# Attention with memory and a two-layer block on one core: more load buffers, and another split of the first queries' preparation over the engines

## The chip, the core and the metric

The kernel runs on one core of a Trainium2 chip. The core has TensorE (PE in the profile) for matrix products, VectorE (DVE), ScalarE (ACT) and GpSimd (POOL) for work on elements, and SyncE (SP), whose queue issues most of the transfers. The metric is the device time of one execution in microseconds, as the median of several runs.

## What is computed

Four batches, eight heads, 576 tokens, head width 64. The output of attention, 2304 tokens of 512 values, passes through a two-layer block with 2048 hidden values.

```python
scores = where(causal, -1e9, q @ k.T / 8);  a = softmax(scores);  local = a @ v
q_p = where(q > 0, q, exp(q) - 1) + 1
mem_out = (q_p @ M_prev) / (q_p @ z_prev + 1e-6)
g = 1 / (1 + exp(-beta))
x = g * mem_out + (1 - g) * local          # (4, 576, 8*64) in all
h = x @ w_in
out = (h * sigmoid(1.702 * h)) @ w_out
```

## The kernel before

Heads are handled in pairs: two heads of 64 channels fill 128 partitions, and a batch has four pairs, 16 pairs in all. Attention of the 16 pairs, the first product of the block (x by `w_in`, 16 blocks of 128 columns, 8 chunks of tokens) and the second product (with `w_out`) follow each other on TensorE, with the first product's matmuls filling in between those of attention.

*The first queries.* `first_queries` (L286) handles the first 256 queries of batch 0 for all four pairs at once, so that the block has a first chunk x to work on early. It loads keys and queries (`fk`, `fq`, `fv`, `fm`, `fz`: keys and queries transposed, queries, values, memory, normaliser). `score` computes scores, their row maximum (VectorE, L541) and exp (ScalarE, L547). `norm` (L339) scales the exp by the reciprocal of their sum, one head on GpSimd and one on VectorE (L550), transposes them on TensorE (L351 to L353) and copies them out on ScalarE into `ft`. `phi` (L361) computes q_p: ScalarE makes exp(-relu(-q)) into `fqm`, and max(q, 0) is added to it, for two pairs on VectorE in one operation (L369), for the other two on GpSimd in two (L368, L370); then q_p is multiplied by z, for two pairs on VectorE, for two on GpSimd. `phin` (L380) sums that over the channels, takes the reciprocal and divides q_p by it, again two pairs on each engine. `mscale` (L375) multiplies the memory by the gate g, one operation a pair on GpSimd. `qtr` transposes the divided queries and copies them to `fqt`; `values` (L400) multiplies everything with memory and values, and `split_sum` turns the result into the two parts `xh` and `xl` of x. The order of calls is norm(0), phi, norm(1), phin, norm(2), norm(3), mscale, qtr, values.

*The weights.* A block of `w_in` comes as pairs of 32-bit words of a 64-bit number (`wraw`, 512 KB). `conv_unit` (L200) loads it, scales it on ScalarE (L213), puts the bits together in three VectorE operations (L224, L229, L231) and splits the result into `wi` (ScalarE, L236, and GpSimd, L241). The raw words of the 16 blocks use the buffers named by the letters in `conv_in` (L268): `c` has two of its own, `e` two of a pool used later for `w_out`, `h` and `l` those of x of later batches. Blocks 0 to 3 are loaded at the start, the others at slots before their place in `CONV`. The decoding of block 0 is told to stay behind the division of pair 1 and the last VectorE scaling (`state["bits"]`).

*The rest of the pairs.* Work is put into slots by `at(slot, priority, fn)`; pair p begins at slot `K0[p]` (7 or 8 slots apart). `load_kq` and `load_vq` issue the transfers of a pair on SyncE's queue: keys and queries transposed (`kqf`, two buffers), values (`vr`, two buffers), memory, queries and normaliser (`mr`, `qr`, `zb`, pool `ldp`, one buffer each). `plan_prep` computes q_p from `qr` in `qmin` and `qexp` (ScalarE, L489, L492), `qphi` (VectorE, L496), `zmul` (GpSimd), `norm` and `smul`, and scales the memory in `mplain`. Within a queue or engine instructions run in the order in which a planner puts them when the program is built; it weighs readiness by a model of time and the priorities, and `add_manual_dep` with `NOSYNC` fixes the order of two instructions on one engine. The planner orders the whole program at once.

Of the kernel before, what the change touches and what calls it, by code (L numbers as in the profile page):

```python
# [34 lines left out]
def tile_attention_memory_moe(ctx, tc, kq, vq, mem, zz, beta, w_in, w_out, out):  # L35
# [29 lines left out]
    mox = pool(attn, "mox", 2, side="right")  # L65
    ldp = pool(attn, "ldp", side="right")
    att = pool(attn, "att", side="right")
    wkp = pool(attn, "wkp", side="right")
    sml = pool(attn, "sml", 6, side="right")
    ps_s = pool(attn, "ps_s", 4, space=PSUM, side="right")  # L70
    ps_x = pool(attn, "ps_x", 1, space=PSUM, side="right")
# [196 lines left out]
    def conv_in(blk):  # L268
        w = w1[blk].tile([128, 2, DM], F32R, name=f"wi{blk}")
        if blk < AHEAD:  # L270
            wb[blk] = w
        raw = {
            "c": (cnv, {"bufs": 2}), "e": (ear[0], {"tag": "r"}),
            "h": (mop, {"tag": "xh"}), "l": (mop, {"tag": "xl"})}["cceehlcchleeccee"[blk]]
        ws = (lambda: ps_o, {"tag": "po"}) if blk == 3 else (lambda: ps_x, {"tag": "ps"})
        parts = conv_unit(None, w, w_in[blk], *raw, *ws, att, {"tag": f"qpt{blk % 2}", "bufs": 2})
        if blk < AHEAD:
            return parts

        c = CONV[blk - AHEAD]  # L280
        at(max(c - 6, -7), 58, parts[0])
        for fn in parts[1:]:
            at(c, 58, fn)
        at(c + 3, 1, lambda: wb.update({blk: w}))

    def first_queries(b):  # L286
# [74 lines left out]
        def phi(behind):  # L361
# [4 lines left out]
            nc.scalar.activation(out=w, in_=w, func=AF.Exp, scale=-1.0)  # L366
            v, p = slice(0, NP), slice(NP, 2 * NP)
            nc.gpsimd.tensor_scalar(out=qv[:, p], in0=qv[:, p], scalar1=0.0, scalar2=None, op0=ALU.max)  # L368
            nc.vector.scalar_tensor_tensor(out=qv[:, v], in0=qv[:, v], scalar=0.0, in1=w[:, v], op0=ALU.max, op1=ALU.add)  # L369
            tt("P", qv[:, p], qv[:, p], w[:, p], ALU.add)  # L370
            for c in range(NP):
# [3 lines left out]
        def mscale(c):  # L375
            x = nc.gpsimd.tensor_scalar(
                out=m[:, c], in0=m[:, c], scalar1=gt[:, c:c + 1], scalar2=None, op0=ALU.mult)
            tc.add_manual_dep(x.ins, box["n", min(c + 1, 3)], NOSYNC, reason="fm")

        def phin():  # L380
            n = fst.tile([128, NP, 2, 2, 1], F32, name="fn")
            nv = n.rearrange("p c t h o -> p (c t) h o")
            nc.vector.tensor_reduce(out=nv[:, :, :, 0], in_=qm, op=ALU.add, axis=AX.X)
            nc.vector.reciprocal(out=n, in_=n)
            for c in range(NP):
                w = q[:, c].rearrange("p t (h d) -> p t h d", h=2)
                box["q", c] = tt("VP"[c // 2], w, w, n[:, c].to_broadcast([128, 2, 2, D]), ALU.mult).ins.name

# [31 lines left out]
        norm(1)  # L420
        phin()
        norm(2)
        norm(3)
        state["bits"] = (box["q", 1], box["v", 3])
        for c in range(NP):
# [25 lines left out]

    def load_vq(p):
        b, c = pairs[p]

        vr = att.tile([128, 5, 128], F32, name="vr", bufs=2)
        nc.sync.dma_start(vr, vq[b, c, :, 0])
        mr = ldp.tile([128, 2, D], F32, name="mr")
# [5 lines left out]
        nc.sync.dma_start(zb, zz[b, c:c + 1, :].to_broadcast([128, 128]))  # L463
        raws[p].update(v=vr, m=mr, q=qr, z=zb)

# [5 lines left out]
    def plan_prep(p):  # L471
# [62 lines left out]
        if p + 1 < len(pairs):  # L534
            at(K0[p + 1] - 11, 60, lambda: load_kq(p + 1))
            at(max(K0[p + 1] - 8, s0 + 8), 60, lambda: load_vq(p + 1))

# [275 lines left out]
    load_kq(0)  # L813
    load_vq(0)
    for p in range(NPAIRS):
# [326 lines left out]
```

## Time and profile before

| what | us |
|---|---|
| median of 3 runs (615.55 to 618.78) | 615.9 |
| the profiled execution, its own time | 616.93 |
| its span from first to last instruction | 615.2 |
| TensorE busy | 593.0 (96%) |
| VectorE busy | 421.7 (69%) |
| ScalarE busy | 347.9 (57%) |
| GpSimd busy | 214.9 (35%) |

All times in the rows below are counted from the start of the profiled span. An engine that is busy all the time sets the pace of its stretch; where it stands, the view of waits tells what it stood for. The granted clock is TensorE's, as a share of 2.4 GHz. A wait that several things end is put down to the one that came last.

### The profile page before, as it was taken

The numbers are of one execution on the slowest core, as the hardware profiler recorded it, in microseconds if no ns is written. First come the engines' busy times: TensorE is split into PE (matmuls) and PEld (weight loads), VectorE is DVE, ScalarE is ACT, GpSimd is POOL, SyncE is SP. The second block draws the span as 40 slices with busy tenths as digits, with TensorE's granted clock in tenths as the row PEclk, the third lists the DMA queues.
The fourth block names the chain that finished last, engine by engine and source line by source line (L and its number), as shares of the span: only waits on it lengthen the run. The fifth ranks groups of instructions, "written<-read, shape, count | busy, mean of one in ns | idle before, by whom it ended". The sixth has DMA issues, their size and how long they took to land.

```text
span 615.2 us, 11404 instructions
## 1 busy us (share of the span) xinstructions
PE 593.0 (96%) x4000; PEld 518.4 (84%) x4000; DVE 421.7 (69%) x1022; ACT 347.9 (57%) x811; POOL 214.9 (35%) x279
## 2 busy tenths in 40 slices
PE   5789999999999999999999999999999999999997
PEld 3467767777787888787788889999999999999997
DVE  5877986666667576676565434679688679766964
ACT  6776766555557355365454343465686865576441
POOL 4765665543536235344334231213412401220000
PEclk9598999999999999999999999999999999999999
DMA  8784442433255355365342126522544733471002
GB/s 261 266 282 119 164 140 92 133 125 104 71 178 189 91 173 173 85 198 151 108 135 66 54 74 221 194 92 75 182 149 138 250 118 75 144 245 52 26 1 77
DMA packets 46985, 84.11 MB, mean 137 GB/s; under 512 B 5328, under 2 KB 33232, under 8 KB 46928
## 3 DMA queue, kind: packets, MB, share of 16 engines
q1 hardware_dynamic: 40688, 61.36, 30.5%
q0 software_dynamic: 6240, 22.02, 11.5%
q8 instruction: 31, 0.51, 0.4%
q14 instruction: 26, 0.21, 0.1%
HBM read 59.77 MB, written 23.59 MB: 136 GB/s over the span
## 4 chain that ended last, share of the span: by engine, by line
PE 68%; DVE 10%; issue 6%; DMA 6%; ACT 5%; POOL 3%; SPq 0%; DVEq 0%; POOLq 0%; ACTq 0%
PE pm L129 22%; PE acc L994 20%; PE ps L129 9%; PE pt L138 8%; PE po L129 8%; DVE wo L151 2%; DMA g<-gd 2%; DMA qr<-in_vq_dram 2%; POOL g L937 2%; ACT a L547 2%; DVE ps L541 1%; DVE st L151 1%; DMA wraw<-in_w_out_dram 1%; DMA wraw<-in_w_in_dram 1%; DVE ol L151 1%
## 5 line engine op out<-in xcount | busy, mean ns | idle before, releaser
L129 PE MATMUL pm<-xh,wi 128*128 128x320 f32 (+1 forms) x1024 | 219.7, 305 | 1.5 <-POOL wi L151 1.4
L129 PEld LDWEIGHTS pm<-xh,wi 128*128 128x128 f32 x1024 | 165.5, 190 | 7.5 <-POOL wi L151 2.7
L994 PE MATMUL acc<-oh,wo 128*128 128x384 f32 x672 | 169.6, 336 | 0.7 <-ACT hk L143 0.7
L129 PE MATMUL pm<-xl,wi 128*128 128x256 f32 (+1 forms) x512 | 152.1, 298 | 0.1
L994 PEld LDWEIGHTS acc<-oh,wo 128*128 128x128 f32 x672 | 121.4, 188 | 1.3 <-ACT hk L143 1.0
L550 POOL TENSOR_SCALAR a<-a,sm,g 128x512 f32<-128x512 f32 (+3 forms) x112 | 76.3, 693 | 129.4 <-DVE sm L601 97.6
L994 PE MATMUL acc<-ol,wo 128*128 128x384 f32 x336 | 111.0, 337 | 0.4 <-DVE ol L151 0.4
L151 DVE TENSOR_TENSOR ol<-g,oh 128x768 fp32r<-128x768 f32 x84 | 79.6, 954 | 40.1 <-ACT oh L143 39.8
L129 PEld LDWEIGHTS pm<-xl,wi 128*128 128x128 f32 x512 | 96.9, 190 | 0.5 <-DVE xl L151 0.3
L547 ACT ACTIVATE a<-ps,nm 128x256 f32<-128x256 f32 (+2 forms) x112 | 59.7, 539 | 64.2 <-DVE nm L541 64.1
L143 ACT ACTIVATE oh<-g 128x768 fp32r<-128x768 f32 x84 | 69.8, 842 | 43.6 <-PE acc L994 31.7
L541 DVE CUSTOM_DVE_ANT_0 ps<-ps,mask 128x256 f32<-128x256 f32 (+4 forms) x144 | 67.3, 506 | 39.0 <-PE ps L129 38.2
L129 PE MATMUL ps<-kqf 128*128 128x288 f32 (+4 forms) x288 | 71.0, 477 | 3.0 <-ACT at L547 1.4
L937 POOL DMA_DIRECT2D g<-gd x48 | 34.8, 726 | 99.4 <-DVE ol L151 76.7
L994 PEld LDWEIGHTS acc<-ol,wo 128*128 128x128 f32 x336 | 62.8, 188 | 0.9 <-DVE ol L151 0.9
L143 ACT ACTIVATE hk<-pm 128x256 f32<-128x256 f32 (+1 forms) x76 | 30.7, 408 | 41.4 <-PE pm L129 37.6
L138 PE MATMUL pt<-ident,a 128*128 128x128 f32 x296 | 53.5, 274 | 0.1
L943 ACT ACTIVATE g<-g 128x768 f32<-128x768 f32 x48 | 39.5, 838 | 18.4 <-DMA g<-gd 15.7
L129 PEld LDWEIGHTS po<-e,vr 128*64 128x64 f32 x416 | 29.9, 137 | 20.1
L151 DVE TENSOR_TENSOR g<-g,g 128x768 f32<-128x768 f32 x48 | 45.4, 950 | 1.4 <-ACT g L943 1.4
L129 PE MATMUL po<-e,vr 128*64 128x320 f32 (+3 forms) x416 | 45.4, 359 | 0.0
L129 PEld LDWEIGHTS ps<-kqf 64*128 64x128 f32 (+1 forms) x288 | 30.3, 189 | 15.1 <-issue 5.3
(126 smaller groups left out, 774.7 us busy)
## 6 DMA issues: line engine op xcount, KB each, us to landing
g<-gd POOLq DMA_DIRECT2D x48, 384.0 KB, 4.8
gd<-hk SPq DMA_DIRECT2D x64, 160.0 KB, 1.9
wraw<-in_w_in_dram SPq DMA_DIRECT2D x16, 512.0 KB, 5.2
gd<-hk SPq DMA_DIRECT2D x64, 128.0 KB, 1.8
kqf<-in_kq_dram SPq DMA_DIRECT2D x12, 608.0 KB, 5.8
vr<-in_vq_dram SPq DMA_DIRECT2D x16, 320.0 KB, 4.9
wraw<-in_w_out_dram SPq DMA_DIRECT2D x10, 512.0 KB, 4.0
qr<-in_vq_dram SPq DMA_DIRECT2D x12, 320.0 KB, 3.0
```

The source lines that it names most:

```text
L129: x = nc.tensor.matmul(out, l, r, start=start, stop=stop)
L138: state["att"] = nc.tensor.transpose(out, in_, idn).ins.name
L143: return nc.scalar.activation(out=dst, in_=src, func=AF.Copy, **kw)
L151: return (nc.vector if eng == "V" else nc.gpsimd).tensor_tensor(out=dst, in0=a, in1=b, op=op)
L541: nc.vector.tensor_tensor_reduce(out=ps, in0=ps, in1=mk, op0=ALU.add, op1=ALU.min, scale=-0.125, scalar=1e38 if j == 0 else nm[:, j - 1:j] ...
L547: return nc.scalar.activation(out=a, in_=ps, func=AF.Exp, scale=-1.0, bias=nm, accum_out=sm)
L550: return (nc.vector if eng == "V" else nc.gpsimd).tensor_scalar(out=a, in0=a, scalar1=r, scalar2=gcol, op0=ALU.mult, op1=ALU.mult)
L937: x = nc.gpsimd.dma_start(t, gd[4 * kh + p][:, :, t0:t0 + QN].rearrange("i p t -> p i t"))
L943: x = nc.scalar.activation(out=t, in_=t, func=AF.Gelu_apprx_sigmoid)
L994: nc.tensor.matmul(acc[b, j][:, :QN], W[2 * p + kk][:, WPART[i], sp, 128 * j:128 * j + 128], mv[:, kk], start=first and p + kk == 0 and sp ...
```

## The change

- The pool `ldp` (memory, queries, normaliser of a pair) gets two buffers of each in place of one.
- A new pool `raws_f` has two buffers for raw weight words. Blocks 6, 7, 14 and 15 use it; blocks 10 and 11 go from `e` to `c`, 12 and 13 from `c` to `e`.
- In `phi` VectorE does max and add of both halves, the half that GpSimd goes on with first.
- `mscale` runs on ScalarE, told to stay behind the last copy of transposed scores.
- `phin` works by halves, the first behind the VectorE scaling of pair 2, the second behind that of pair 3, and is called after norm(3).
- `load_vq` is divided: `load_v` stays at its slot, `load_q` (memory, queries, normaliser) comes with `load_kq`, three slots earlier for most pairs.

```diff
--- before.py
+++ after.py
@@ -63,10 +63,11 @@
     ps_m = pool(left, "ps_m", 2, space=PSUM, side="left")
     dr = pool(ctx, "dr", space=bass.MemoryType.DRAM)
     mox = pool(attn, "mox", 2, side="right")
-    ldp = pool(attn, "ldp", side="right")
+    ldp = pool(attn, "ldp", 2, side="right")
     att = pool(attn, "att", side="right")
     wkp = pool(attn, "wkp", side="right")
     sml = pool(attn, "sml", 6, side="right")
+    raws_f = pool(attn, "raws_f", 2, side="right")
     ps_s = pool(attn, "ps_s", 4, space=PSUM, side="right")
     ps_x = pool(attn, "ps_x", 1, space=PSUM, side="right")
     ps_o = pool(attn, "ps_o", 1, space=PSUM, side="right")
@@ -271,7 +272,8 @@
             wb[blk] = w
         raw = {
             "c": (cnv, {"bufs": 2}), "e": (ear[0], {"tag": "r"}),
-            "h": (mop, {"tag": "xh"}), "l": (mop, {"tag": "xl"})}["cceehlcchleeccee"[blk]]
+            "h": (mop, {"tag": "xh"}), "l": (mop, {"tag": "xl"}),
+            "f": (raws_f, {"tag": "f"})}["cceehlffhlcceeff"[blk]]
         ws = (lambda: ps_o, {"tag": "po"}) if blk == 3 else (lambda: ps_x, {"tag": "ps"})
         parts = conv_unit(None, w, w_in[blk], *raw, *ws, att, {"tag": f"qpt{blk % 2}", "bufs": 2})
         if blk < AHEAD:
@@ -364,27 +366,28 @@
             x = nc.scalar.activation(out=w, in_=qv, func=AF.Relu, scale=-1.0)
             tc.add_manual_dep(x.ins, behind, NOSYNC, reason="phi")
             nc.scalar.activation(out=w, in_=w, func=AF.Exp, scale=-1.0)
-            v, p = slice(0, NP), slice(NP, 2 * NP)
-            nc.gpsimd.tensor_scalar(out=qv[:, p], in0=qv[:, p], scalar1=0.0, scalar2=None, op0=ALU.max)
-            nc.vector.scalar_tensor_tensor(out=qv[:, v], in0=qv[:, v], scalar=0.0, in1=w[:, v], op0=ALU.max, op1=ALU.add)
-            tt("P", qv[:, p], qv[:, p], w[:, p], ALU.add)
+            for p in (slice(NP, 2 * NP), slice(0, NP)):
+                nc.vector.scalar_tensor_tensor(
+                    out=qv[:, p], in0=qv[:, p], scalar=0.0, in1=w[:, p], op0=ALU.max, op1=ALU.add)
             for c in range(NP):
                 tt("VP"[c // 2], w[:, 2 * c:2 * c + 2], qv[:, 2 * c:2 * c + 2],
                    z[:, c:c + 1, :].rearrange("p o (h d) -> p o h d", h=2).to_broadcast([128, 2, 2, D]), ALU.mult)
 
         def mscale(c):
-            x = nc.gpsimd.tensor_scalar(
-                out=m[:, c], in0=m[:, c], scalar1=gt[:, c:c + 1], scalar2=None, op0=ALU.mult)
-            tc.add_manual_dep(x.ins, box["n", min(c + 1, 3)], NOSYNC, reason="fm")
+            x = copy("A", m[:, c], m[:, c], gt[:, c:c + 1])
+            tc.add_manual_dep(x.ins, state["first", 0], NOSYNC, reason="fm")
 
         def phin():
             n = fst.tile([128, NP, 2, 2, 1], F32, name="fn")
             nv = n.rearrange("p c t h o -> p (c t) h o")
-            nc.vector.tensor_reduce(out=nv[:, :, :, 0], in_=qm, op=ALU.add, axis=AX.X)
-            nc.vector.reciprocal(out=n, in_=n)
-            for c in range(NP):
-                w = q[:, c].rearrange("p t (h d) -> p t h d", h=2)
-                box["q", c] = tt("VP"[c // 2], w, w, n[:, c].to_broadcast([128, 2, 2, D]), ALU.mult).ins.name
+            for k in range(2):
+                x = nc.vector.tensor_reduce(
+                    out=nv[:, NP * k:NP * k + NP, :, 0], in_=qm[:, NP * k:NP * k + NP], op=ALU.add, axis=AX.X)
+                tc.add_manual_dep(x.ins, box["v", 2 + k], NOSYNC, reason="norm")
+                nc.vector.reciprocal(out=n[:, 2 * k:2 * k + 2], in_=n[:, 2 * k:2 * k + 2])
+                for c in (2 * k, 2 * k + 1):
+                    w = q[:, c].rearrange("p t (h d) -> p t h d", h=2)
+                    box["q", c] = tt("VP"[k], w, w, n[:, c].to_broadcast([128, 2, 2, D]), ALU.mult).ins.name
 
         def qtr(k):
             if not k:
@@ -418,9 +421,9 @@
         norm(0)
         phi(box["e", 1])
         norm(1)
-        phin()
         norm(2)
         norm(3)
+        phin()
         state["bits"] = (box["q", 1], box["v", 3])
         for c in range(NP):
             mscale(c)
@@ -449,11 +452,13 @@
             nc.sync.dma_start(kqr, kq[b, c])
         raws[p] = {"kq": kqr}
 
-    def load_vq(p):
+    def load_v(p):
         b, c = pairs[p]
-
-        vr = att.tile([128, 5, 128], F32, name="vr", bufs=2)
+        vr = raws[p]["v"] = att.tile([128, 5, 128], F32, name="vr", bufs=2)
         nc.sync.dma_start(vr, vq[b, c, :, 0])
+
+    def load_q(p):
+        b, c = pairs[p]
         mr = ldp.tile([128, 2, D], F32, name="mr")
         nc.sync.dma_start(mr, mem[b * NP + c])
         qr = ldp.tile([128, 5, 128], F32, name="qr")
@@ -461,7 +466,7 @@
         nc.sync.dma_start(qr[:, t:], vq[b, c, :, 1, t:])
         zb = ldp.tile([128, 128], F32, name="zb")
         nc.sync.dma_start(zb, zz[b, c:c + 1, :].to_broadcast([128, 128]))
-        raws[p].update(v=vr, m=mr, q=qr, z=zb)
+        raws[p].update(m=mr, q=qr, z=zb)
 
 
     def hold(p, x):
@@ -533,7 +538,8 @@
         at(s0 + 13, 31, qev)
         if p + 1 < len(pairs):
             at(K0[p + 1] - 11, 60, lambda: load_kq(p + 1))
-            at(max(K0[p + 1] - 8, s0 + 8), 60, lambda: load_vq(p + 1))
+            at(K0[p + 1] - 11, 60, lambda: load_q(p + 1))
+            at(max(K0[p + 1] - 8, s0 + 8), 60, lambda: load_v(p + 1))
 
     def softmax_max(pieces):
         nm = sml.tile([128, 2], F32, name="nm")
@@ -811,7 +817,8 @@
     first.close()
     w1.update({k: pool(left, f"w1_{k}", side="left", reuse_waits="tile") for k in range(W0, NB - 2)})
     load_kq(0)
-    load_vq(0)
+    load_v(0)
+    load_q(0)
     for p in range(NPAIRS):
         plan_prep(p)
         plan_attend(p)
```

## Rows read from the trace of the kernel before

**Rows 1.** The page: busy time by engine, and granted clock in 40 slices

```profile
PE 593.0 (96%) x4000; PEld 518.4 (84%) x4000; DVE 421.7 (69%) x1022; ACT 347.9 (57%) x811; POOL 214.9 (35%) x279
...
PEclk9598999999999999999999999999999999999999
```

**Rows 2.** Stretches: length, busy us of PE, PEld, DVE, ACT, POOL, granted clock, DMA share, GB/s

```profile
13.50:17.40 3.90, 0.27 (x2) 0.03 (x1) 3.71 (x16) 3.89 (x16) 3.66 (x4) 0.60 1.04 405
17.40:22.50 5.10, 3.41 (x12) 1.98 (x12) 3.22 (x9) 2.66 (x7) 5.10 (x9) 0.50 1.05 368
22.50:28.00 5.50, 5.21 (x14) 3.17 (x14) 5.38 (x14) 3.71 (x10) 2.37 (x4) 0.50 0.60 199
...
36.00:42.00 6.00, 5.78 (x44) 5.38 (x44) 6.00 (x19) 4.02 (x10) 4.12 (x6) 1.00 0.95 311
42.00:48.00 6.00, 4.06 (x19) 2.26 (x18) 3.14 (x9) 4.37 (x12) 4.41 (x6) 1.00 0.72 263
48.00:52.00 4.00, 4.00 (x21) 3.72 (x20) 2.42 (x6) 2.50 (x7) 1.44 (x2) 0.57 0.01 4
...
100.00:375.00 275.00, 272.88 (x2036) 223.67 (x2036) 165.20 (x553) 137.45 (x414) 109.98 (x137) 1.00 0.40 125
375.00:615.00 240.00, 235.64 (x1448) 233.95 (x1442) 178.04 (x241) 141.35 (x210) 42.63 (x50) 1.00 0.38 123
```

**Rows 3.** Waits of TensorE: waited for, us in total, times, longest us

```profile
PE pt L351 <- DVE fa L550: 4.6, 2, 3.7
```

**Rows 4.** Order of time, TensorE, 43 to 46 us: start, length, operation, idle before

```profile
43.31 0.39 PE L129 MATMUL pm<-xh,wi 128*128 128x256 f32 x1 [1.02 <-POOL wi L151]
...
45.91 1.12 PE L129 MATMUL ps<-kqf 64*128 64x512 f32 x2 [0.92 <-ACT at L547]
```

**Rows 5.** Order of time, ScalarE, at 22, 23 and 43 us

```profile
21.95 0.60 ACT L143 ACTIVATE ft<-pt 128x512 f32<-128x512 f32 x1 [2.19 <-PE pt L352]
...
23.12 0.40 ACT L143 ACTIVATE ms<-mr,gt 128x128 f32<-128x128 f32 x1
...
43.09 0.53 ACT L489 ACTIVATE qmt<-qr 128x384 f32<-128x384 f32 x1 [1.86 <-DMA qr<-in_vq_dram]
```

**Rows 6.** The chain that ended last, around 36 us: start, length, what

```profile
36.26 6.81 DMA qr<-in_vq_dram
```

**Rows 7.** Order of time, GpSimd, 14 to 20.4 us

```profile
14.24 1.73 POOL L368 TENSOR_SCALAR fq<-fq 128x512 f32<-128x512 f32 x1
16.06 1.17 POOL L151 TENSOR_TENSOR fq<-fq,fqm 128x512 f32<-128x512 f32 x1
...
19.01 1.40 POOL L151 TENSOR_TENSOR fqm<-fq,fz 128x256 f32<-128x256 f32 x2
```

**Rows 8.** Order of time, VectorE, 13.9 to 26.9 us

```profile
13.93 0.69 DVE L369 SCALAR_TENSOR_TENSOR fq<-fq,fqm 128x512 f32<-128x512 f32 x1 [0.17 <-ACT fqm L366]
...
20.45 1.24 DVE L383 TENSOR_REDUCE fn<-fqm 128x16 f32<-128x1040 f32 x1 [1.55 <-POOL fqm L151]
21.72 0.25 DVE L384 RECIPROCAL fn<-fn 128x16 f32<-128x16 f32 x1
...
26.31 0.56 DVE L507 TENSOR_REDUCE nrm<-qmt 128x6 f32<-128x390 f32 x1
```

**Rows 9.** Groups by form, VectorE, 13 to 24.5 us: count, busy us, mean ns, idle before

```profile
L151 DVE TENSOR_TENSOR fq<-fq,fn 128x256 f32<-128x256 f32 x2 | 1.4, 734 | 0.0
...
L151 DVE TENSOR_TENSOR fqm<-fq,fz 128x256 f32<-128x256 f32 x2 | 0.8, 421 | 0.0
```

**Rows 10.** Groups by form, GpSimd, 13 to 24.5 us and the whole span

```profile
L376 POOL TENSOR_SCALAR fm<-fm,gt 128x128 f32<-128x128 f32 x4 | 2.5, 630 | 0.4 <-DMA fm<-in_mem_dram 0.4
...
L550 POOL TENSOR_SCALAR a<-a,sm,g 128x512 f32<-128x512 f32 x32 | 27.6, 872 | 58.6 <-DVE sm L601 41.1 <-ACT r L844 14.9 <-ACT hk L143 2.6
```

**Rows 11.** Waits of ScalarE and of SyncE's queue for and behind qr, whole span

```profile
ACT qmt L489 <- DMA qr<-in_vq_dram: 12.0, 5, 3.8
...
SPq L461 <- DVE qp L496: 51.5, 10, 9.5
```

## The prediction

> **What bounds the kernel now.** I read four views in this order: the engines' shares on the page, the stretches by stage, the waits of TensorE, and the order of time on each engine around the few waits that last. The page says that TensorE is busy 593.0 of 615.2 us, at full granted clock nearly throughout, but not in the second and fourth slice of some 15 us [rows 1]. The stretches show where the rest lies. From 100 to 375 us TensorE is busy 272.88 of 275 us and from 375 us on 235.64 of 240 us, at granted clock 1.00 [rows 2]: there it is the bound, and a faster VectorE or an earlier load brings at most the 2.1 us that are idle in the first of these two. What can be won lies before. From 13.5 to 17.4 us TensorE works 0.27 of 3.90 us, from 17.4 to 22.5 us 3.41 of 5.10 us, and both that stretch and the next, to 28 us, run at granted clock 0.50, the 1.2 GHz level [rows 2]. From 42 to 48 us 1.94 of 6.00 us are idle, and the stretch behind it, to 52 us, runs at 0.57 on average, mostly the low level again [rows 2]. Since TensorE is saturated later, a microsecond that it loses before 100 us is paid at the end, and one that it gets back there is won at the end.
>
> What TensorE waits for is named by its waits: first the scaled scores of the first queries, 3.7 us at once [rows 3]; then a weight block at 43.31 us (1.02 us) and the exp of a tail at 45.91 us (0.92 us) [rows 4]. Behind the last one stands ScalarE, which stood still 1.86 us until 43.09 us for qr, the queries of the third pair [rows 5]. That transfer was issued at 36.26 us and landed 6.81 us later [rows 6], in a stretch in which the DMA engines are 95% busy; VectorE is full there too, 6.00 of 6.00 us from 36 to 42 us [rows 2]. So the front is a chain over VectorE and GpSimd, and from 36 us on over VectorE, ScalarE and the loads.
>
> **The change, part by part.** *(a) phi, norm and division of the first queries.* Before, GpSimd runs the max of its half (1.73 us), the add (1.17 us), two smaller operations and the two z products (1.40 us), one behind the other to 20.4 us [rows 7], and VectorE stands 1.55 us before the sum of norms at 20.45 us because of them [rows 8]. The change takes max and add from GpSimd (2.90 us) and puts one more scalar_tensor_tensor of 128x512 on VectorE: 0.69 us, the row of the half that already runs there [rows 8]. GpSimd's half goes first, so its products can start near 14.6 us instead of 19.01 us; the sum need not wait for them any more, and the 1.55 us go. The sum and its reciprocal are done by halves: two reduces of 520 elements in place of one of 1040 (1.24 us), and one reciprocal more (0.25 us at full size). A reduce of 390 elements took 0.56 us [rows 8], so one of 520 is 0.69 us on the line between the two, and the split costs 0.14 + 0.25 = 0.39 us, or 0.27 us with reciprocals half as long; I take 0.27 us. VectorE up to its last division is then 1.55 - 0.69 - 0.27 = 0.59 us earlier. Further, its two divisions lasted 734 ns each beside GpSimd's, while two products of the same shape and operation took 421 ns [rows 9]; with the halves apart in time 2 x 313 ns = 0.63 us come back. I take -1.2 us. Bounds: +1.1 us (idle time comes back elsewhere and the added 0.69 + 0.39 us stay) and -2.2 us (1.55 + 0.63 us, the added work lying in other idle time). The norms of pairs 2 and 3 now stand ahead of the queries' sum on VectorE, so the transposes of scores are not pushed back by it. What follows on VectorE is the decoding of the first weight block, which waits for its divisions; and since VectorE is full from 36 to 42 us, the same amount should arrive at the weight block of 43.31 us.
>
> *(b) Memory scaling on ScalarE.* Four operations of 630 ns leave GpSimd [rows 10] and come to ScalarE, where one of this shape takes 0.40 us [rows 5]: 1.6 us, behind the copy of the last pair's transposed scores. ScalarE stands 2.19 us just before that copy [rows 5], and the copy comes earlier if (a) holds, so I cost it at 0. If that cover is gone, the copy of the transposed queries, queued behind, is 1.6 us later, and all of x with it: bounds 0 and +1.6 us.
>
> *(c) Two buffers for queries, memory and normaliser of a pair, loaded earlier.* On SyncE the load of qr waits for VectorE's last read of the pair before, 51.5 us in 10 cases [rows 11], and holds back what is issued behind it: the other loads and the stores. With a second buffer, and an issue planned three slots earlier, the third pair's qr goes out before the burst of 36 us. ScalarE's 1.86 us go, and TensorE's 0.92 us at 45.91 us with them: -0.9 us (bounds 0, if the burst only moves, and -1.9 us, if all of ScalarE's standing was on the path). ScalarE's other waits for qr, 12.0 - 1.86 = 10 us in four cases [rows 11], I cost at 0: after 100 us TensorE runs through.
>
> *(d) The low clock behind it.* If idle time between 42 and 48 us falls from 1.94 to about 1.0 us, the low stretch behind it should go: 4.00 us at mean 0.57 lose 4.00 x 0.43 = 1.7 us against the full level [rows 2]. I take all of it, -1.7 us, since the small holes that follow later leave the clock at 1.00 [rows 2]; the other end is 0.
>
> *(e) Own buffers for raw words of four blocks.* The loads of blocks 6 and 7 need not wait until blocks 0 and 1 are decoded, and can fill the stretch from 22.5 to 28 us, where the DMA engines are 60% busy, in place of that from 36 to 42 us at 95% [rows 2]. It supports (c); decoding is bound by VectorE, so by itself 0. Bounds: -1.0 us (the whole wait at 43.31 us goes) and +0.9 us (a load that is now ahead in the queue makes one more wait like that at 45.91 us) [rows 4]. The new buffers also shift the addresses beside them; the stage after 375 us takes over that place long after its last use: 0.
>
> Sum: -1.2 + 0 - 0.9 - 1.7 + 0 = -3.8 us. The profiled run took 616.93 us, 1.7 us more than its span, and 1.0 us more than the median of 615.9 us; against the median the forecast is 612.1 us.
>
> **A rule to weigh.** GpSimd's max of 128x512 took 1.73 us while VectorE ran two-operand work [rows 7, 8]; a scaling of 128x512 on the same engine takes 872 ns on average [rows 10]. The Trainium skill, "SBUF — State Buffer", section "SBUF: two separate sides", says that a VectorE instruction with two SBUF inputs and a GpSimd instruction lock each other out of a shared port pair for its whole length. By that rule, the trace agrees (1.73 us against 872 ns, 734 against 421 ns), and it speaks against (a): the 0.69 us moved to VectorE would stand in GpSimd's way as well.
>
> **Rivals.** *R1: VectorE takes the place of GpSimd.* The two engines stretch each other as before, VectorE has about 1 us more to do and was nearly full already: (a) gives 0, the 1.02 us at 43.31 us stay, and with them enough idle time for the low clock. Left is (c): 615.9 - 0.9 = 615.0 us. For it speaks VectorE's 6.00 of 6.00 us; against it, its 1.55 us of idle time, which GpSimd alone explains. *R2: the front becomes longer, and the kernel slower.* Place: ScalarE between the last pair's copy and that of the transposed queries, near 22 to 24 us; it decides from the point at which the first queries are transposed before the four scalings are through. Then x is 1.6 us later, VectorE's 1.0 us come on top: +2.6 us; the longer hole lengthens the low clock by as much, at half speed +1.3 us: 615.9 + 3.9 = 619.8 us. Against it speaks the 2.19 us of idle time before. *R3: the buffers don't do what they say.* SyncE issues in order, and the DMA engines count as over 100% busy up to 22.5 us [rows 2]: qr lands no earlier than before, and (a) alone stays: 614.7 us. *R4: more comes back.* (a) at -2.2 us, (c) at -1.9 us, the dip's -1.7 us and (e) at -1.0 us: 615.9 - 6.8 = 609.1 us.
>
> **How the numbers follow.** About 0.5%, 3.1 us, is what a measurement of this kernel can tell from no change: faster means under 612.8 us, slower over 619.0 us. Forecast 0.50, own range 610.5 to 614 us, of which 0.40 falls under 612.8 us; R1 0.22; R3 0.06; R2 0.12, of which 0.09 over 619.0 us; R4 0.10. So faster 0.50, same 0.41, slower 0.09. The range of 8 in 10 runs from 608.0 us, a little beyond R4, to 617.5 us and leaves out R2.
>
> **What would show it.** (a): no idle time of VectorE before the sum of norms, divisions near 421 ns, x complete 1 us sooner. (b): four scalings on ScalarE ahead of the copy of the queries, and no wait of TensorE for that copy. (c): qr of the third pair issued before 32 us, and no wait of ScalarE for it. (d): granted clock 1.00 from 46 to 52 us. From 100 us on both traces should run in step at a constant distance. What would make it wrong: a new wait of TensorE after 60 us, since the order of instructions is planned anew for the whole kernel, or a low clock elsewhere.

## The result, and the profile after

The changed kernel takes 612.15 us (median of 10 runs, 609.09 to 616.18), the kernel before 617.17 us beside it (median of 10, 615.55 to 619.12): ratio 0.9912, 95% interval 0.9888 to 0.9936. It is faster, by 5.0 us between the medians, and 612.1 us was the forecast, which counted from 615.9 us. The profiled execution took 612.23 us, its span is 610.5 us, 4.7 us under that of before.

The page of the changed kernel, the two lines that answer to [rows 1]:

```profile
PE 588.4 (96%) x4000; PEld 515.7 (84%) x4000; DVE 421.9 (69%) x1025; ACT 348.8 (57%) x815; POOL 210.8 (35%) x273
...
PEclk9799999999999999999999999999999999999999
```

TensorE does the same 4000 matmuls in 4.6 us less busy time, and the low slice at 46 to 61 us is gone. Its idle time is the same as before in sum, 22.1 for 22.2 us: it moved, and the gain stands in the busy time. The stretches at the low level of 1.2 GHz that the trace shows up to 600 us, two before and one after (length, busy us of PE, PEld, DVE, ACT, POOL, granted clock, DMA share, GB/s):

```profile
14.31:27.97 13.66, 8.60 (x26) 5.16 (x26) 11.64 (x32) 9.42 (x28) 10.48 (x14) 0.50 0.86 307
48.45:51.86 3.41, 3.41 (x18) 3.41 (x18) 2.20 (x5) 2.05 (x6) 0.99 (x1) 0.50 0.02 5
```

```profile
17.54:24.37 6.83, 5.39 (x21) 4.23 (x22) 5.79 (x17) 4.72 (x15) 3.76 (x6) 0.50 0.93 310
```

So 12.0 us of TensorE's work ran at the low level before and 5.4 us after; at half the clock that is, as an estimate from these rows, 3.3 of the 4.6 us. The stretches of the changed kernel, against [rows 2] (columns as above):

```profile
13.50:17.40 3.90, 0.47 (x3) 0.20 (x2) 3.73 (x14) 3.90 (x15) 2.18 (x3) 1.00 1.02 402
17.40:22.50 5.10, 3.52 (x15) 3.04 (x16) 5.10 (x17) 3.00 (x9) 2.91 (x5) 0.51 1.01 343
22.50:28.00 5.50, 5.50 (x31) 3.14 (x31) 3.69 (x10) 5.50 (x18) 1.69 (x3) 0.83 0.91 338
28.00:36.00 8.00, 7.72 (x59) 5.00 (x56) 7.72 (x24) 6.85 (x18) 6.33 (x8) 1.00 0.84 267
36.00:42.00 6.00, 4.67 (x29) 3.33 (x28) 5.48 (x16) 5.44 (x16) 4.11 (x5) 1.00 1.01 390
42.00:48.00 6.00, 5.92 (x43) 4.94 (x44) 4.89 (x13) 4.18 (x13) 4.66 (x6) 1.00 0.50 168
48.00:52.00 4.00, 3.52 (x28) 2.65 (x28) 3.58 (x8) 2.35 (x6) 2.78 (x3) 1.00 0.47 154
100.00:375.00 275.00, 273.47 (x2047) 225.29 (x2044) 166.97 (x553) 137.20 (x411) 108.44 (x135) 1.00 0.39 125
```

GpSimd has 2.18 us of work in the first stretch where it had 3.66, VectorE no idle time in the second. From 42 to 48 us TensorE stands 0.08 us instead of 1.94 us, but much of that only lies in the neighbouring stretches now: from 36 to 52 us it stands 1.89 us instead of 2.16 us. From 48 to 52 us the granted clock is 1.00 instead of 0.57. TensorE's order of time (start, length, operation, idle before), against [rows 4]:

```profile
42.08 0.38 PE L130 MATMUL pm<-xh,wi 128*128 128x256 f32 x1 [1.05 <-POOL wi L152]
...
43.68 1.13 PE L130 MATMUL ps<-kqf 64*128 64x512 f32 x4
...
51.02 0.92 PE L130 MATMUL ps<-kqf 64*128 64x384 f32 x4 [0.48 <-ACT e L144]
```

The wait for a weight block stays, as long as before (1.05 us), but ends at 42.08 us instead of 43.31 us. The scores behind it start at 43.68 us without a wait, 2.23 us sooner, and the next pair's at 51.02 us. ScalarE in order of time, against [rows 5], and the issue of the third pair's qr on SyncE's queue, against [rows 6]:

```profile
22.41 0.97 ACT L144 ACTIVATE fm<-fm,gt 128x128 f32<-128x128 f32 x3
...
23.55 0.39 ACT L144 ACTIVATE fm<-fm,gt 128x128 f32<-128x128 f32 x1
...
38.08 0.53 ACT L494 ACTIVATE qmt<-qr 128x384 f32<-128x384 f32 x1 [0.39 <-DVE nrm L512]
```

```profile
27.29 0.33 SPq L466 DMA_DIRECT2D qr<-in_vq_dram  x1
```

That transfer was issued at 36.26 us before. ScalarE now starts the third pair's queries 5.0 us sooner (38.08 for 43.09 us), and no transfer holds it up. The waits over the whole span (waited for, us in total, times, longest), against [rows 3, 11]:

```profile
PE pt L353 <- DVE fa L556: 5.3, 2, 4.2
```

```profile
ACT qmt L494 <- DVE nrm L512: 18.3, 8, 3.2
```

```profile
SPq L466 <- DVE qp L501: 51.9, 10, 9.5
```

TensorE's longest wait at the front, for scores that VectorE scales, is longer than before, 4.2 for 3.7 us: VectorE comes to them 1.2 us later (17.73 for 16.49 us). ScalarE's 12.0 us of waiting for qr are gone; what it waits for there now is the sum of the pair before, whose buffer is single (18.3 us in all, for 24.9 us with qr's share before). SyncE's queue waits as long for VectorE as before, 51.9 for 51.5 us: the second buffer did not shorten its waits, it moved them to times when ScalarE does not stand for what is behind. VectorE and GpSimd at the front, against [rows 7, 8]:

```profile
18.36 0.68 DVE L384 TENSOR_REDUCE fn<-fqm 128x8 f32<-128x520 f32 x1
...
19.31 0.76 DVE L152 TENSOR_TENSOR fq<-fq,fn 128x256 f32<-128x256 f32 x2
...
20.63 0.68 DVE L384 TENSOR_REDUCE fn<-fqm 128x8 f32<-128x520 f32 x1
```

```profile
15.05 2.06 POOL L152 TENSOR_TENSOR fqm<-fq,fz 128x256 f32<-128x256 f32 x2 [1.44 <-DVE fq L370]
```

The 1.55 us before VectorE's sum are gone, and its two divisions take 0.76 us together for 1.39 us. GpSimd's z products start at 15.05 us instead of 19.01 us, and take 2.06 us instead of 1.40 us.

**Where the time comes back**, as the time of the same step in both traces (for x its end, for the others the start), before minus after:

| step | before | after | gained |
|---|---|---|---|
| last part of x complete | 36.02 | 34.76 | 1.26 |
| weight block waited for | 43.31 | 42.08 | 1.23 |
| scores behind it | 45.91 | 43.68 | 2.23 |
| scores of the next pair | 55.71 | 51.02 | 4.69 |
| scores, the pair behind | 121.98 | 117.85 | 4.13 |
| transposes | 190.76 | 186.56 | 4.20 |
| span | 615.2 | 610.5 | 4.7 |

Nearly all is decided by 52 us. Of the 4.7 us gained by then 0.6 us are lost again at a wait of TensorE that before has not (0.60 us, to 59.93 us), a small case of the sign that the prediction named as speaking against it. From 118 to 187 us both traces run at a constant distance; a 0.51 us wait of before at 292.75 us has no counterpart after, and gives the rest.

### The profile page after: what moved, and what is told of

Read it like the earlier page. It is cut to its first block, busy times and chain, and to the rows that moved or that the text cites. A ratio compares the mean times of both kernels' runs of the same rounds, so it can differ in the third digit from the quotient of the medians.

```text
span 610.5 us, 11390 instructions
## 1 busy us (share of the span) xinstructions
PE 588.4 (96%) x4000; PEld 515.7 (84%) x4000; DVE 421.9 (69%) x1025; ACT 348.8 (57%) x815; POOL 210.8 (35%) x273
## 4 chain that ended last, share of the span: by engine, by line
PE 74%; DVE 10%; DMA 6%; issue 5%; ACT 2%; POOL 2%; SPq 1%; DVEq 0%; POOLq 0%; ACTq 0%
PE pm L130 28%; PE acc L1001 21%; PE pt L139 8%; PE ps L130 8%; PE po L130 8%; DVE wo L152 2%; DMA g<-gd 2%; DMA qr<-in_vq_dram 2%; POOL g L944 2%; DVE ps L547 1%; DMA fv<-in_vq_dram 1%; DVE st L152 1%; ACT a L553 1%; DVE ws L230 1%; DVE ol L152 1%
## 5 line engine op out<-in xcount | busy, mean ns | idle before, releaser
L130 PE MATMUL ps<-kqf 128*128 128x288 f32 (+4 forms) x288 | 69.1, 473 | 2.9 <-ACT at L553 1.2
L144 ACT ACTIVATE e<-pt 128x320 f32<-128x320 f32 (+2 forms) x76 | 32.7, 435 | 20.1 <-PE pt L139 15.8
```

The source lines that it names most:

```text
L130: x = nc.tensor.matmul(out, l, r, start=start, stop=stop)
L144: return nc.scalar.activation(out=dst, in_=src, func=AF.Copy, **kw)
```

## The experiments

Twelve kernels, each timed in five rounds beside the kernel before on the same chip:

| kernel | median us | ratio | 95% interval |
|---|---|---|---|
| loads_only | 611.81 | 0.9935 | 0.9908 to 0.9961 |
| front_only | 615.66 | 1.0000 | 0.9977 to 1.0024 |
| one_qr | 617.55 | 1.0039 | 1.0011 to 1.0067 |
| after_again | 610.85 | 0.9918 | 0.9889 to 0.9946 |
| qr_two | 613.14 | 0.9937 | 0.9913 to 0.9961 |
| no_f | 610.67 | 0.9904 | 0.9877 to 0.9930 |
| phi_pool | 611.14 | 0.9911 | 0.9886 to 0.9937 |
| mscale_pool | 613.67 | 0.9956 | 0.9937 to 0.9974 |
| qr_ms | 610.20 | 0.9886 | 0.9862 to 0.9910 |
| warm | 614.43 | 0.9962 | 0.9942 to 0.9982 |
| phin_whole | 612.38 | 0.9925 | 0.9897 to 0.9953 |
| pool_hold | 612.48 | 0.9928 | 0.9904 to 0.9952 |

The kernel before took 616.13 us beside the first four, 616.71 us beside the next four, 617.27 us beside the next three, and 616.1 us beside the last.

### Two halves, one buffer taken away, and the change again

*loads_only*: the kernel before with the load half of the change (`ldp` with two buffers, `raws_f` and the letters, `load_v` and `load_q`). *front_only*: the other half (`phi`, `mscale`, `phin`, its call after norm(3)). *one_qr*: the changed kernel with one line different:

```diff
-        qr = ldp.tile([128, 5, 128], F32, name="qr")
+        qr = ldp.tile([128, 5, 128], F32, name="qr", bufs=1)
```

*after_again*: the changed kernel, nothing different.

> The kernel before with the load part of the change alone: two buffers of memory, queries and normaliser, loaded with the keys, and own buffers for the raw words of four blocks; phi, norm, division and memory scaling as before. My theory (the gain has two sources that add): the front is as before, x complete near 36.0 us, the weight block near 43.3 us still waited for, but ScalarE no longer waits 1.86 us for the third pair's queries, TensorE's 0.92 us near 45.9 us go, and the low clock from 48.4 to 51.9 us with them: 2.8 us under the kernel before, ratio 0.9955. Rival A (the front does it all): no difference, ratio 1.000. Rival B (the loads do it all): the whole 5 us, ratio 0.991.

> The kernel before with the work part of the change alone: max and add of phi on VectorE, memory scaling on ScalarE, norm and division by halves and later; loads and buffers as before. My theory: x complete 1.2 us sooner and the weight block of 43.31 us near 42.1 us, but ScalarE still stands for the third pair's queries and the low clock near 48 us comes again: 1.2 us under the kernel before, ratio 0.998. Rival A: the whole 5 us, ratio 0.991. Rival B: nothing, 1.000, because the time that the front gives back is waited for at the queries' landing instead.

> The changed kernel with one buffer for the queries of a pair again (memory and normaliser keep two, the raw words their own buffers). My theory: the third pair's queries go out only after VectorE's last read of the second pair's, near 34.5 us, land into the burst of raw words near 40 us, and ScalarE and TensorE wait again, by about 1 us, with a low clock behind: 1 to 2.8 us over the changed kernel, ratio against the kernel before 0.9935 to 0.9965. Rival (the raw words' buffers thin out the burst and do what I put down to the queries' second buffer): as the changed kernel, 0.991.

> The changed kernel, unchanged, timed beside the others on the same chip, with a second profile. Expected: ratio 0.991 against the kernel before, no low clock after 30 us. The low clock at the front lasted 6.83 us in the first profile and 13.65 us in that of the kernel before; if that length is a matter of the run, it differs here, and the span with it by about 1 us; if it belongs to the kernel, it is 6.8 us again.

The loads alone give 0.65% and the front alone nothing; without qr's second buffer the changed kernel is slower than the kernel before, by more than was expected; why it falls behind the kernel before stays open. The interval of front_only reaches down to 0.9977, which leaves room for the 1.2 us expected of it. Why the front alone gives so little is in its trace. The profiled execution of front_only is the longest of its twelve, so its order and waits are read here, not its span. ScalarE, then TensorE:

```profile
40.70 0.52 ACT L490 ACTIVATE qmt<-qr 128x384 f32<-128x384 f32 x1 [2.24 <-DMA qr<-in_vq_dram]
```

```profile
41.80 0.39 PE L129 MATMUL pm<-xh,wi 128*128 128x256 f32 x1 [1.91 <-ACT wi L143]
```

x is complete at 34.75 us there, as in the changed kernel, but qr, issued at 34.44 us, lands 6.18 us later, and ScalarE and then TensorE stand for it. What the front had won is waited for again, and behind the wait the clock is low from 44.10 to 54.34 us. In one_qr it is the same: qr, issued at 34.37 us, lands at 40.34 us, TensorE stands 1.69 us before 41.51 us, and behind that the clock is low from 42.32 to 45.73 us. So the halves don't add: the front's gain has to pass through a wait that only the buffer removes. That the front adds anything to the loads is not shown by these runs: loads_only and after_again, timed in the same rounds, lie 1.0 us apart, and their intervals overlap.

### qr's second buffer alone, and without the raw-word buffers

*qr_two* is the kernel before with `bufs=2` in that one line (memory and normaliser keep one buffer, the load its old slot). *no_f* is the changed kernel with the letters and buffers of the raw weight words as before:

```diff
-            "f": (raws_f, {"tag": "f"})}["cceehlffhlcceeff"[blk]]
+            }["cceehlcchleeccee"[blk]]
```

> The kernel before with one thing changed: two buffers for the queries of a pair; all loads keep their slots, memory, normaliser and raw words keep their buffers, the first queries' work is as before. Theory (the wait for the third pair's queries is the largest single term): they are issued before the second pair's are read, land before ScalarE comes to them, and TensorE's 0.92 us near 45.9 us and the low clock behind go: 2.6 us or more under the kernel before, ratio 0.993 to 0.996. Rival (it takes the earlier issue or the thinner burst as well): the transfer still lies behind the raw words of blocks 5 and 6 in SyncE's order and lands after 41 us; no difference, ratio 1.000.

> The changed kernel without the own buffers for raw words: letters of the blocks as before, no pool for them. Theory (decoding is bound by VectorE, the raw words' buffers bring nothing by themselves): as the changed kernel, ratio against the kernel before 0.991 to 0.993, weight block near 42.1 us as there. Rival (the thinner burst is what lets the queries land in time): ScalarE waits for the third pair's queries again, 1 to 3 us over the changed kernel, ratio 0.994 to 0.997.

One word in one line gives 0.9937, as much as the whole load half; the raw-word buffers give nothing (0.9904 without them). ScalarE and TensorE in qr_two:

```profile
39.18 0.53 ACT L489 ACTIVATE qmt<-qr 128x384 f32<-128x384 f32 x1
```

```profile
43.18 0.39 PE L129 MATMUL pm<-xh,wi 128*128 128x256 f32 x1 [1.05 <-POOL wi L151]
...
52.12 0.92 PE L129 MATMUL ps<-kqf 64*128 64x384 f32 x4 [0.48 <-ACT e L143]
```

The weight block comes no sooner than before (43.18 for 43.31 us), but the next pair's scores start 3.6 us sooner (52.12 for 55.71 us): between these two marks lay the 0.92 us wait and the low clock of 3.4 us, and both are gone.

### phi and the memory scaling back on GpSimd, one at a time

*phi_pool*: the changed kernel with phi's GpSimd half as before. *mscale_pool*: the changed kernel with this alone:

```diff
-            x = copy("A", m[:, c], m[:, c], gt[:, c:c + 1])
-            tc.add_manual_dep(x.ins, state["first", 0], NOSYNC, reason="fm")
+            x = nc.gpsimd.tensor_scalar(
+                out=m[:, c], in0=m[:, c], scalar1=gt[:, c:c + 1], scalar2=None, op0=ALU.mult)
+            tc.add_manual_dep(x.ins, box["n", min(c + 1, 3)], NOSYNC, reason="fm")
```

> The changed kernel with max and add of GpSimd's half of phi back on GpSimd. Theory: GpSimd's products end 2 us later, VectorE stands before the second half of the sum of norms, x is complete near 35.5 us instead of 34.8 us, the weight block comes 1 us later: 1 us over the changed kernel, ratio against the kernel before 0.9935. Rival (VectorE is the bound at the front, so the 0.65 us of the added operation come back): as the changed kernel or a little under, 0.990 to 0.992.

> The changed kernel with the memory scaling back on GpSimd. ScalarE has 1.4 us less between 22.4 and 24 us, just ahead of the copies of the transposed queries, and GpSimd, which stands 2.5 us in all between 17 and 22.2 us, has 2.5 us more. Theory (the move costs and brings nothing): x complete within 0.3 us of the changed kernel, ratio 0.991 to 0.992. Rival (on ScalarE it lies in the way of the copies of the transposed queries, as was feared): x complete 1 us sooner than in the changed kernel, ratio 0.990.

Taking phi's second half to VectorE is worth nothing that can be told (0.9911 without it, 0.9912 with it), as the rival had it, though x is complete only at 37.33 us in phi_pool: when x is complete does not by itself set the time. The scalings, which were costed at nothing, are worth 2.8 us between the medians of mscale_pool and after_again, which ran on two chips, and 2.3 to 2.7 us by the ratios; the interval of mscale_pool begins at 0.9937, where that of the changed kernel ends at 0.9936, and overlaps that of after_again, which ends at 0.9946.

### The smallest edit: qr's buffer and the scalings on ScalarE

*qr_ms* is the kernel before with `bufs=2` for qr and `mscale` on ScalarE: three lines. (What its expectation calls the second pair's queries are the first that `plan_prep` prepares, from the first `qr`; and the scalings are tied behind the first of the two copies of the last pair's transposed scores.)

> The kernel before with two changes alone: a second buffer for the queries of a pair (qr), and the four memory scalings on ScalarE, tied behind the first copy of the transposed keys as in the changed kernel. qr's second buffer alone gave 0.9937 (613.1 us beside 616.7 us); in the changed kernel the scalings on GpSimd instead of ScalarE cost 2.8 us (0.9956 beside 0.991). Theory A: the scalings' place is worth its 2.8 us wherever it is, because ScalarE then does them before the second pair's queries, which otherwise push themselves ahead of x on VectorE and TensorE: 610.5 us or so, 0.989 to 0.991, as good as the whole change, with a fraction of its lines. Theory B: the 2.8 us come only together with the new order on VectorE (phi and norms), and without it the scalings on ScalarE are hidden as they were costed: 613 us, 0.992 to 0.995, and the start of the second pair's queries on ScalarE stays where it is in the kernel with qr's buffer alone. Theory C, the prediction's second rival: on ScalarE without the faster front they hold up the transposed queries by up to 1.6 us: 614.5 us, 0.996 or more.

It gives 0.9886 (610.20 us, all six runs from 609.62 to 610.39), at least as much as the whole change, so theory A holds in its number; the trace shows a second reason beside A's. GpSimd and VectorE in qr_two, then in qr_ms:

```profile
18.44 0.74 POOL L376 TENSOR_SCALAR fm<-fm,gt 128x128 f32<-128x128 f32 x1
19.15 1.40 POOL L151 TENSOR_TENSOR fqm<-fq,fz 128x256 f32<-128x256 f32 x2
```

```profile
20.59 1.24 DVE L383 TENSOR_REDUCE fn<-fqm 128x16 f32<-128x1040 f32 x1 [1.55 <-POOL fqm L151]
```

```profile
17.90 1.46 POOL L151 TENSOR_TENSOR fqm<-fq,fz 128x256 f32<-128x256 f32 x2
```

```profile
19.79 1.23 DVE L382 TENSOR_REDUCE fn<-fqm 128x16 f32<-128x1040 f32 x1
```

Two of the four scalings stand on GpSimd ahead of the z products (0.60 us before phi's max and 0.74 us just before them). With these gone the products end 1.2 us sooner and VectorE's 1.55 us of idle time are gone, without one more operation on VectorE. x is complete at 33.81 us for 35.86 us, the third pair's queries start at 37.26 us for 39.18 us, and at the mark of 118.87 us the gain is 1.55 us. The other half of the 2.9 us between the medians stands in neither trace: the spans are 609.9 and 608.5 us. The clock changes too. The low level at the front, in qr_two and then in qr_ms (columns as above):

```profile
17.27:27.51 10.24, 7.99 (x25) 5.15 (x26) 8.24 (x20) 5.99 (x15) 7.74 (x13) 0.50 0.88 295
```

```profile
16.58:23.40 6.82, 4.59 (x18) 3.63 (x19) 6.62 (x18) 5.36 (x16) 5.15 (x8) 0.50 1.02 342
```

TensorE does 3.4 us less of its work at the low level; half of that, 1.7 us as an estimate, is as much as the traces gain. That the place of the scalings is worth the time is shown; how the gain divides between GpSimd's relief, ScalarE's order and the clock is not.

### Is it GpSimd's time or ScalarE's order?

*pool_hold* is mscale_pool with the first `qmt` of the main loop tied behind the copy of `fqt` on ScalarE:

```diff
+            if p == 0:
+                tc.add_manual_dep(x.ins, box0["fqt"], NOSYNC, reason="after fqt")
```

> The changed kernel with the memory scalings back on GpSimd (which took 0.9956, 2.8 us more than the changed kernel), and beside that the first exp of the main loop's first pair (the first qmt from qr) tied on ScalarE behind the second copy of the transposed first queries (fqt). In the trace with the scalings on GpSimd that first qmt starts at 22.39 us, 1.45 us sooner than in the changed kernel, GpSimd's divisions start at 22.16 us in both, and x is complete 1.5 us later, TensorE having done other scores ahead of it and at the low clock to 26.2 us. Theory A: what the scalings cost on GpSimd is the order that the freed ScalarE takes up, not GpSimd's time: with the order held back the kernel is as fast as the changed one, 0.990 to 0.993 (611 to 612 us). Theory B: GpSimd's 2.5 us themselves cost it: 0.995 or above, as without the tie. Theory C: the tie delays the first pair, and that costs as much as it gives: 0.994 to 0.998 with x complete by 35 us.

That first `qmt` on ScalarE, in mscale_pool and in pool_hold:

```profile
22.39 0.52 ACT L495 ACTIVATE qmt<-qr 128x384 f32<-128x384 f32 x1
```

```profile
25.59 0.52 ACT L496 ACTIVATE qmt<-qr 128x384 f32<-128x384 f32 x1
```

With it held back, x is complete at 34.39 us instead of 36.29 us, and the ratio is 0.9928: in the range of theory A, but its interval reaches those of both neighbours. In the changed kernel, where phi no longer loads GpSimd, the scalings hold up nothing there: GpSimd's divisions end at 23.34 us in mscale_pool and at 23.35 us in the changed kernel. What else differs is the order that the planner gives to a ScalarE that is free at 22.4 us, and the clock: the low level at the front ends at 26.18 us in mscale_pool, at 23.40 us in pool_hold and at 24.37 us in the changed kernel. That the order makes the 2.8 us is possible, not settled.

### The norms undivided

*phin_whole* is the changed kernel with the sum, reciprocal and divisions of `phin` as before.

> The changed kernel with the sum of norms, its reciprocal and the divisions undivided, as in the kernel before, in the place of the divided ones. Theory A (the prediction's term): the halves win what VectorE and GpSimd no longer take from each other in the divisions, 0.6 us, less 0.3 us for one more sum and reciprocal; x is complete up to 0.5 us later without them, and of that nothing that a ratio can tell reaches the end: 0.990 to 0.993. Theory B: the halves let VectorE begin its part of the division 2 us before GpSimd's, and the weight decode behind it too; without them the first weight block and with it everything to 42 us is 1 us or more later: 0.994 or above. Theory C: the added sum and reciprocal are a loss, and the undivided form is faster: 0.989 or below.

0.9925 with x complete at 35.25 us for 34.76 us: theory A. What the halves bring is too small to be told.

### TensorE kept busy at the front

*warm* adds 36 transposes of the identity on TensorE, in `norm(1)` and `norm(2)`, into a part of a PSUM tile that is not read.

> The changed kernel with 36 transposes of the identity more on TensorE in its idle time from 14 to 22 us, into a part of a PSUM tile that nothing reads: work that only keeps TensorE busy. The changed kernel runs 6.8 to 10.2 us of its front at the low granted clock, and over the executions of one kernel the time rises by about 0.4 us for each us of full-speed time that the clock takes away. Theory A: the front's low clock costs time: with TensorE busy in the gap the low stretch is shorter or lies earlier, x is complete before 34 us, and the kernel takes 609 to 610 us (ratio 0.987 to 0.989). Theory B: the front is a chain over VectorE, GpSimd and ScalarE, and TensorE's clock there costs nothing: ratio 0.991, as the changed kernel, low stretch shorter or not. Theory C: the transposes stand in front of the score transposes on TensorE and take their own time, up to 2 us: 612.5 us or more, 0.993 and above.

It took 614.43 us, a ratio in theory C's range, but doesn't settle what the clock costs. The granted clock is 1.00 from 13.5 to 25.5 us, and then low from 25.55 to 32.38 us, mostly over work without idle time. And the plan came out another way. ScalarE at the front, and the stretch from 28 to 36 us (columns as above):

```profile
23.37 0.63 ACT L214 ACTIVATE ws<-wraw 128x512 f32<-128x512 f32 x1 [3.33 <-DVE wr L232]
23.94 0.58 ACT L144 ACTIVATE ft<-pt 128x512 f32<-128x512 f32 x1
```

```profile
28.00:36.00 8.00, 8.00 (x47) 4.21 (x47) 5.78 (x13) 4.89 (x15) 4.79 (x5) 0.73 0.79 270
```

A copy of weight words was put ahead of the scores' copy on ScalarE and waited 3.33 us for VectorE; the copy came at 23.94 us for 21.91 us, x at 38.14 us. Two causes, and the run can't part them.

## Why the prediction was right

**(a) phi, norm and division: -1.2 us.** The signs named for it are all there: no idle time before the sum of norms, divisions of 424 ns on average (forecast 421), x 1.26 us sooner, and the same 1.23 us at the weight block. But the credit went to the wrong edit. phi's half on VectorE is worth nothing that can be told (phi_pool), and qr_ms has the same VectorE idle time removed with phi as it was. The prediction read the 1.55 us as made by GpSimd's max and add. Two scalings of the memory stood in the same chain [rows 7], in the trace of before:

```profile
13.66 0.60 POOL L376 TENSOR_SCALAR fm<-fm,gt 128x128 f32<-128x128 f32 x1 [0.39 <-DMA fm<-in_mem_dram]
...
18.31 0.73 POOL L376 TENSOR_SCALAR fm<-fm,gt 128x128 f32<-128x128 f32 x1
```

One runs just ahead of the max, the other just ahead of the z products. The first it left out, the second was one of its "two smaller operations". And the gain holds only with (c): front_only is 1.0000. The sum also has no term for the clock at the front, where the low level ends at 24.37 us for 27.97 us. The transposes of the divided queries start 0.8 us sooner (21.88 for 22.68 us, at the low level in both), which is the chain's gain; how the 1.26 us at x divide between the chain and the clock is open.

**(b) Scalings on ScalarE: 0, bounds 0 and +1.6 us.** This is the term that was mis-sized. It measures -2.3 to -3.1 us (mscale_pool against the changed kernel, 0.9956 to 0.9918 and 0.9912; qr_two to qr_ms, 0.9937 to 0.9886). The prediction costed what arrives on ScalarE and not what the four operations of 630 ns [rows 10] free on GpSimd, and so left a gain out of the bounds without a reason. By which way the gain comes, relief, order or clock, is open. The cover that it named held: in qr_ms the second copy of fqt ends at 25.49 us for 27.69 us in qr_two.

**(c) and (d) qr's second buffer and the low clock: -0.9 and -1.7 us.** Together -2.6 us; qr_two measures -3.6 us between medians, and 3.1 us at the mark of 118.87 us. In the changed kernel the table gives 1.0 us for (c), the step from 1.23 to 2.23 us, and 2.5 us more up to 51.02 us, of which the low clock of 3.4 us at half the level is 1.7 us. Of the rest 0.6 us are lost again at 59.93 us. No experiment changes the clock alone there, so (d) is shown as going with (c), not as a price of its own: the low stretch stands behind TensorE's idle time in before (1.02 and 0.92 us), front_only (1.91 and 0.75 us) and one_qr (1.69 and 0.76 us), and is absent in after, qr_two and loads_only, where one wait of about 1.05 us is left. It is absent in warm as well, where TensorE waits 0.76 us before 45.02 us and 0.98 us before 46.75 us, so that the shorter idle time alone keeps the level up is not shown.

**(e) Raw-word buffers: 0.** Right: no_f is as fast.

**The sum.** -3.8 us forecast, -5.0 us between the medians. That 612.15 us stands so near to 612.1 us is luck: the gain was 1.2 us larger, and the kernel before came out 1.3 us slower than the 615.9 us counted from. The whole change is 1.5 us better than qr_two by the ratios, with overlapping intervals, where (a) and (b) had 1.2 us; the scalings alone bring more in qr_ms, so that of the front's edits only they are shown to bring anything, and the gain was booked under (a). (c) and (d) are right in mechanism, and about 1 us larger. That the parts depend on each other did not show in the forecast, since all were made at once.

**The rivals.** R1, VectorE as the new bound, fell in its time: x came sooner, and VectorE has 0.3 to 1.8 us of idle time in each of the five stretches from 22.5 to 52 us. But its ground is real. From 17.4 to 22.5 us VectorE has no idle time, TensorE waits 4.2 us for it, and the move of phi's half brings nothing that can be told. GpSimd's two z products took 2.06 us for 1.40 us, and VectorE's two, for the most part at the same time, 686 ns on average for 421 ns [rows 9]. By the rule of the Trainium skill, "SBUF — State Buffer", section "SBUF: two separate sides", a VectorE instruction with two SBUF inputs and a GpSimd instruction that reads SBUF lock each other out of a shared port pair for the whole of an instruction; the trace agrees in that both become longer, 2.06 against 1.40 us. That one is held for the whole of the other's length is not what the rows show, as far as GpSimd's spans go: before, VectorE's two z products (15.02 to 15.78 us, 421 ns on average) ran inside GpSimd's max (14.24 to 15.97 us), and only the max was long. So the 421 ns, from which the prediction counted, are not those of a VectorE that works alone. What the longer products cost is not shown; VectorE had hardly a wait to fill there, 0.17 us from 13.5 to 17.4 us and none in the stretch behind. R2 fell: the four scalings lie on ScalarE ahead of the copies of fqt, and the first of these ends 0.35 us later (25.13 for 24.77 us), but the second 1.0 us sooner (26.57 for 27.55 us), and x with it. R3 fell: qr is issued 9.0 us sooner. R4's 609.1 us is the lowest of the ten runs of the changed kernel, and within 1.1 us of qr_ms.

## What to carry to other kernels

When work moves from one engine to another, cost what it frees on the engine it leaves, at the place where it stood: find each instruction that runs there ahead of the one that somebody waits for. Gains at the front of a kernel are kept only if the next thing on the path is early too; test the halves of a change by themselves before adding them up. Here a second buffer for one tile and four small operations on another engine did as much as the whole change. And see what TensorE does while its clock is low: here the low level cost nothing that can be seen over idle time, and about half its length over work.

## What the runs showed of the hardware that was not expected

The low clock at the front lies elsewhere in two executions of the same program, and in this pair the time doesn't follow. The changed kernel's profile has it from 17.54 to 24.37 us, that of after_again from 14.56 to 24.80 us, at spans of 610.5 and 610.3 us. The first two stretches of after_again (columns as above) show the level of 1.2 GHz for most of the first, where the changed kernel has 1.00:

```profile
13.50:17.40 3.90, 0.44 (x2) 0.20 (x2) 3.73 (x15) 3.90 (x15) 2.08 (x3) 0.64 1.03 404
17.40:22.50 5.10, 3.62 (x16) 3.07 (x16) 5.10 (x16) 3.00 (x9) 3.02 (x5) 0.50 1.01 342
```

VectorE and ScalarE do the same work in the same time in both, and TensorE, which works 0.44 of the first 3.90 us, waits for them: the longer low stretch lies over its idle time. Where it lies over work it costs time. From the transposes of scores at 17 to 18 us up to the weight block the kernel before and loads_only do the same work on TensorE in the same order, but in loads_only the low level ends at 32.26 us for 27.97 us. The stretch from 28 to 36 us, before and then in loads_only:

```profile
28.00:36.00 8.00, 8.00 (x60) 4.41 (x59) 6.63 (x20) 6.58 (x19) 4.80 (x5) 1.00 0.50 169
```

```profile
28.00:36.00 8.00, 8.00 (x46) 4.27 (x47) 4.57 (x12) 4.77 (x14) 4.17 (x4) 0.73 0.50 179
```

TensorE is busy throughout in both and does 46 matmuls for 60. In loads_only x is complete at 38.01 us for 36.02 us, and the weight block starts at 45.33 us for 43.31 us: 2.0 us for 4.3 us more at the low level. That is the half by which the prediction's second rival priced a longer low stretch at the front, 1.3 us for 2.6 us. Over many executions the time goes with the clock too: within one kernel it rises by about 0.4 us for each us of full-speed time that the mean granted clock takes away, wherever in the span (126 executions of before, of the changed kernel and of the first eight experiments; correlation 0.55).
